# A newly searched order of one core's instructions, and warm-up matmuls on a tile of zeros, in a block-sparse attention and feed-forward kernel

## The chip, the cores and the metric

The kernel runs on one core of a Trainium2 chip. The metric is the device time of one execution in microseconds (us); lower is better. The core has several engines, each with its own queue of instructions which it executes in order: TensorE (PE, matrix products, with a separate row PEld for the loading of weights), VectorE (DVE), ScalarE (ACT), GpSimd (POOL) and SyncE (SP, which here only issues DMA transfers). Data come from the chip's memory (HBM) into SBUF by DMA; products land in PSUM.

## The reference

Inputs are q, k and v of shape 4 batches x 8 heads x 768 tokens x 64, and two weights, 512x2048 and 2048x512. Cut to what matters:

```python
k_rep = k.reshape(B, H, n_blocks, 64, D).mean(axis=3)          # 12 blocks of 64 keys
gate_scores = einsum('bhsd,bhnd->bhsn', q, k_rep)              # masked to causal blocks
top_idx = argsort(gate_scores)[..., -3:]                       # 3 best blocks of a query
scores = scale * q @ k.T       # kept only in the chosen blocks and the query's own, causal
attn = softmax(scores)
x = (attn @ v).transpose(0, 2, 1, 3).reshape(3072, 512)
out = gelu_tanh(x @ w_in) @ w_out
```

## The kernel before, in words

The 32 heads are worked on as 16 pairs, p = 0 to 15, four pairs to a batch b. For each pair `load` (L375 on) brings k, q and v by SP's queue: `first` issues one part and `others` the rest, and for pairs from 4 on k and q take four DMAs each (L396) and v two (L390). `pre` prepares a pair: k and q are turned (on TensorE for batch 0, L540 and L543; with DVE's transpose, L559, later), the block sums of k are taken (`ksb_h` L590, or `ks_all` L616 and `ksb_m` L633), the gate is computed by eight small matmuls (`gate`, L682), and DVE picks three blocks (L698, L705 to L719) and builds the additive mask `madd`, which a transpose (L751) or a transposing DMA (`mask_dma`, L758) turns. `heads2` (batch 0) and `heads` (batches 1 to 3) then compute the attention in units: scores into the PSUM tiles `wide` (L858, L1041), ACT's exponential (L877, L1054), POOL's causal cut (L903, L1068), the product with v (L926, L1080) and DVE's division (L944; L963 and L964). `turn_out` turns the result into xT (L983, or a DMA, L988).

The feed-forward of a batch has two stages. `s1` multiplies xT with w_in (L1117, groups of eight matmuls into `wide`, each followed by ACT's gelu, L1129); the last batch uses `s1_seven` (L1206, L1230, L1165). The second stage is a plain product with w_out for batch 0 (`s2_plain`, L1317, stores at L1342) and for the others one with seven block products in place of eight (`s2`, L1367), whose sums and differences DVE forms in the tiles XS and TS (`sums`, L1304; `w_sums`, L1286) and adds up (L1416). The weights come by POOL's DMA queue (`load_w`); an SP instruction, `hold` (L1562), waits for the second half of w_in before pair 4's loads go out. Batch b's second stage shares TensorE with the attention of batch b+1.

`consts` has POOL write constants: the causal tables, and for each of four buffer sets the memsets of `emit_p` (L505 to L509; L507 clears the first 128 columns of mT2[i], the turned masks, whose tiles are parts of XS). An identity matrix is built by POOL, and DVE casts it to `ident16` (L280). `warm` (L1514 on) defines up to 72 warm-up matmuls, 128x128 on 128x256, whose results nobody reads; L1519 in the profile.

None of this runs in the order of the text. Each step is an op, given to a planner with `add`: on which engines it may run, at what cost, behind which ops, with what priority. A search outside of the kernel has used these costs, and its result stands in three tables: ORDER (L21), the list of op numbers in the order in which they are emitted; BUFFER, which of several equal buffers each op takes; ENGINE, which ops go to ACT or POOL when they have a choice (the rest go to the first engine named, mostly DVE). `Plan.run` goes through ORDER and emits op after op. Every engine executes its own ops in that order, and waits inside its queue for whatever an op depends on. The costs themselves emit nothing. Ops 0 to 1889 are the real ones, 1890 on the warm-ups; ORDER holds 26 of these.

Op numbers that the text uses: 974 is `ksb_m` of pair 8, 977 the gate of pair 8, 1039 the DVE transpose of pair 9's q, 1040 the gate of pair 9; 450, 468 and 524 are output stores of batch 0; 408 to 411 are a group of the first stage that reads the second half of w_in; 337 and 338 are the casts of pair 4's k.

Of the kernel before, what the change touches and what calls it, by code (L numbers as in the profile page):

```python
# [9 lines left out]
FP16 = mybir.dt.float16  # L10
# [178 lines left out]
    "POOL": [  # L189
        337, 338, 586, 587, 646, 647, 707, 708, 972, 973, 1035, 1036,  # L190
        1097, 1159, 1160, 1426, 1489, 1613]}


class Op:
# [40 lines left out]
def kernel(  # L235
# [9 lines left out]
    nc = tc.nc  # L245
# [6 lines left out]
    HP = H // 2  # L252
# [1369 lines left out]
```

## Time and profile before

| what | us |
|---|---|
| median of 3 runs | 258.84 (258.12 to 259.08) |
| the profiled execution's own time | 258.29 |
| its span in the trace | 256.6 |
| PE busy in the span | 246.3 (96%) |
| DVE, ACT, POOL busy | 193.6, 174.1, 85.2 |
| first matmul of all starts at | 2.27 |
| first matmul of the feed-forward (L1117) | 37.61 |

The span is 1.7 us shorter than the execution's time; the rest lies around it. In the profile L12 is line 12 of the kernel. A timeline row is: start, duration, engine, line, operation, what it writes and reads, and in square brackets how long the engine had idled before it and what released it. "SPq" is SP issuing a DMA, not the transfer itself. "PEclk" is the granted clock of TensorE in tenths.

### The profile page before, as it was taken

The page shows a single profiled execution, that of the slowest core. Times are in us where ns is not written, and L with a number is a line of the kernel's source. Part 1 is how long each engine was busy: PE and PEld are TensorE (multiplying, and loading weights), DVE is VectorE, ACT ScalarE, POOL GpSimd, SP SyncE. Part 2 cuts the span into 40 slices and gives each one's busy share as a digit, 9 for nine tenths or more (in the row PEclk, how much of TensorE's full clock was granted, in tenths as well). Part 3 has the DMA queues.
Part 4 walks back from the last instruction along what each step waited for, and adds up shares of the span by engine and source line. Part 5 has one row for each costly group of instructions (what it writes and reads, how often), then busy time and mean ns, then how long its engine had stood idle before and what let it go on. Part 6 is the DMA issues. An engine that isn't in the chain of part 4 may idle for free.

```text
span 256.6 us, 6416 instructions
## 1 busy us (share of the span) xinstructions
PE 246.3 (96%) x2472; PEld 171.1 (67%) x2472; DVE 193.6 (75%) x542; ACT 174.1 (68%) x220; POOL 85.2 (33%) x165
## 2 busy tenths in 40 slices
PE   6999999999999996999999999999999999999994
PEld 5766676655455564555777888656777787666883
DVE  1688871032899995998999998998898773668954
ACT  2489886444789896767888874556898956576300
POOL 8448860012055966030173754000075520000000
PEclk9999999999999999999999999999999999999999
DMA  8998599999998998999999994153110321021024
GB/s 162 218 201 171 86 211 188 213 153 151 159 136 143 158 208 124 172 154 225 181 140 206 197 120 79 28 179 100 26 43 2 64 74 41 1 80 45 4 82 164
DMA packets 130927, 32.62 MB, mean 127 GB/s; under 512 B 124528, under 2 KB 126928, under 8 KB 130896
## 3 DMA queue, kind: packets, MB, share of 16 engines
q1 hardware_dynamic: 126160, 27.62, 64.3%
q0 software_dynamic: 3136, 4.19, 9.7%
q10 hardware_dynamic: 1600, 0.39, 0.8%
q8 instruction: 19, 0.31, 0.5%
q14 instruction: 12, 0.10, 0.1%
HBM read 27.26 MB, written 6.29 MB: 131 GB/s over the span
## 4 chain that ended last, share of the span: by engine, by line
PE 69%; DVE 17%; ACT 3%; DMA 3%; issue 2%; SPq 2%; POOL 2%; DVEq 0%; ACTq 0%; POOLq 0%
PE wide L1117 18%; PE bank L1367 17%; PE wide L1041 6%; PE bank L1317 5%; PE wide L1206 5%; PE bank L1080 4%; PE wide L858 3%; DMA sd<-in_q_dram 3%; DVE XS L1304 3%; DVE sel L714 2%; PE bank L682 2%; DVE G L1304 2%; PE bank L926 2%; PE bank L540 2%; DVE qT L363 2%
## 5 line engine op out<-in xcount | busy, mean ns | idle before, releaser
L1117 PE MATMUL wide<-xT,w_in 128*128 128x384 f16 x416 | 73.7, 326 | 0.0
L1054 ACT ACTIVATE ats<-wide 128x896 f16<-128x896 f32 x72 | 62.9, 916 | 8.0 <-PE wide L1041 6.0
L1129 ACT ACTIVATE G<-wide 128x768 f16<-128x768 f32 x52 | 41.9, 810 | 30.5 <-PE wide L1117 30.2
L1117 PEld LDWEIGHTS <-w_in 128*128 128x128 f16 x416 | 40.0, 98 | 26.2 <-issue 1.0
L1068 POOL TENSOR_SCALAR_AFFINE_SELECT ats<-ats 128x256 f16<-128x256 f16 x72 | 33.2, 477 | 68.4 <-ACT ats L1054 67.8
L1041 PE MATMUL wide<-qT,kT 76*128 76x512 f16 (+3 forms) x192 | 38.9, 305 | 0.2 <-ACT ats L1054 0.2
L559 DVE STREAM_TRANSPOSE s<-sd 128x768 f32<-128x768 f32 x24 | 23.2, 968 | 18.5 <-DMA sd<-in_k_dram 13.4
L1367 PE MATMUL bank<-w_out,G 128*128 128x256 f16 x216 | 33.1, 273 | 0.7 <-DVE G L1304 0.3
L1367 PEld LDWEIGHTS <-G 128*128 128x128 f16 x288 | 26.9, 98 | 7.2 <-DVE G L1304 0.8
L1317 PE MATMUL bank<-w_out,G 128*128 128x512 f16 x96 | 27.6, 379 | 0.0
L1080 PEld LDWEIGHTS <-ats 128*128 128x128 f16 x504 | 22.2, 98 | 5.0 <-issue 0.5
L1416 DVE TENSOR_TENSOR osb<-bank,osb 128x512 f32<-128x512 f32 (+1 forms) x38 | 22.4, 593 | 3.5 <-PE bank L1367 1.8
L1080 PE MATMUL bank<-v,ats 128*128 128x65 f16 x504 | 24.1, 194 | 0.4 <-DVE osb L1416 0.4
L1041 PEld LDWEIGHTS <-kT 76*128 76x128 f16 x192 | 17.2, 98 | 10.4 <-issue 1.3
L1367 PE MATMUL bank<-TS,XS 128*128 128x256 f16 x144 | 23.1, 272 | 0.0
L1367 PEld LDWEIGHTS <-XS 128*128 128x128 f16 x216 | 20.0, 97 | 4.2
L877 ACT ACTIVATE ats<-wide 128x1024 f16<-128x1024 f32 (+3 forms) x24 | 20.9, 921 | 2.1 <-PE wide L858 1.0
L361 POOL CAST kT<-s 64x768 f16<-64x768 f32 x18 | 15.3, 854 | 20.9 <-DVE s L559 17.2
L361 POOL CAST v<-vsd 128x768 f16<-128x768 f32 x13 | 11.8, 906 | 20.6 <-DMA vsd<-in_v_dram 20.5
L964 DVE TENSOR_TENSOR xn<-bank,zr 128x384 f16<-128x384 f32 x24 | 13.4, 557 | 0.8
L714 DVE MAX8 sel<-sel 128x8 f32<-128x12 f32 x160 | 13.3, 157 | 0.6
L1317 PEld LDWEIGHTS <-G 128*128 128x128 f16 x96 | 8.8, 97 | 6.3 <-issue 0.8
(119 smaller groups left out, 359.0 us busy)
## 6 DMA issues: line engine op xcount, KB each, us to landing
out_dram<-osb SPq DMA_DIRECT2D x23, 256.0 KB
vsd<-in_v_dram SPq DMA_DIRECT2D x26, 192.0 KB
sd<-in_k_dram SPq DMA_DIRECT2D x48, 96.0 KB
sd<-in_q_dram SPq DMA_DIRECT2D x48, 96.0 KB
w_in<-in_moe_w_in_dram POOLq DMA_DIRECT2D x2, 1024.0 KB, 11.5
w_out<-in_moe_w_out_dram POOLq DMA_DIRECT2D x2, 1024.0 KB, 17.2
G<-in_k_dram SPq DMA_DIRECT2D x4, 192.0 KB
G<-in_q_dram SPq DMA_DIRECT2D x4, 192.0 KB
```

The lines of the kernel that those rows point to most:

```text
L361: nc.gpsimd.tensor_copy(out=out, in_=in_)
L559: nc.vector.transpose(out=T[key + "T32", p], in_=T[key, p].rearrange("p t j -> p (t j)"))
L877: nc.scalar.activation(out=T["at", u][:, :, 0:n], in_=plan.buf[("st",) + u].rearrange("p (h w) -> p h w", h=2)[:, :, 0:n], func=AF.Exp, bi ...
L1041: nc.tensor.matmul(st[:, x:e], kT16[i][h][0:76, s0:s0 + 128], qT16[i][h][0:76, s0 + (x - cb):s0 + (e - cb)], start=True, stop=True)
L1054: nc.scalar.activation(out=T["at", u][:, 0:n], in_=plan.buf[("st",) + u][:, 0:n], func=AF.Exp, bias=0.0, scale=SCALE)
L1068: nc.gpsimd.affine_select(out=dg, in_=dg, compare_op=ALU.is_ge, fill=0.0, base=0, pattern=[[0, 2], [1, 128]], channel_multiplier=-1)
L1080: nc.tensor.matmul(pvv[:, qc, 0:65], at[:, cb + (qc - jc) * 128: cb + (qc - jc + 1) * 128], v16[i][:, jc, h, :], start=(gi == 0 and jc == ...
L1117: nc.tensor.matmul(hps[:, 512 * e:512 * e + HALF], w_in16[:, ci, (2 * j + e) * 128: (2 * j + e + 1) * 128], T["xT", b][:, ci, HALF * h:HAL ...
L1129: nc.scalar.activation(out=G[:, :, h, j, :], in_=plan.buf["hps", b, j, h].rearrange("p (e w) -> p e w", e=2)[:, :, 0:HALF], func=AF.Gelu_a ...
L1317: nc.tensor.matmul(plan.buf["ops", b, ti], G[:, f % 2, 2 * ti // NC, f // 2, ti % (NC // 2) * 128:ti % (NC // 2) * 128 + 128], w_out16[:, ...
L1367: nc.tensor.matmul(dst[:, HD * h:HD * h + HD], FACT[m][0][:, j, t * 128:(t + 1) * 128], FACT[m][1][:, j, :], start=(clear and j == 0), sto ...
L1416: nc.vector.tensor_tensor(out=dst(), in0=src(), in1=other(), op=ALU.add)
```

## The change

The three tables are replaced by those of a search that went on. The real ops are the same 1890, in another order, with other buffer picks and some on other engines; warm-ups grow from 26 to 39. The planner's costs for loads of pairs from 7 on are raised (2.9 for 2.5, 2.0 for 1.77). The warm-up matmuls read `zero16`, a part of XS[2], which the first instruction of VectorE sets to zero, in place of the identity; that part is the one that `emit_p` cleared for i = 3, so POOL leaves this memset out. XS is allocated further up for it. Lines behind that place are some 5 higher in the changed kernel (L540 is L545, L682 is L687, L1117 is L1122, L1519 is L1524).

```diff
 ORDER = [
-    6, 4, 0, 2, 3, 1, 9, 12, 15, 1890, 1891, 1892, 1893, 1894, 1895, 1896,
-    1897, 1898, 1899, 62, 71, 72, 64, 82, 63, 18, 22, 23, 19, 1900, 1901,
-    66, 75, 73, 68, 76, 26, 74, 67, 1902, 1903, 1904, 78, 31, 32, 35, 27,
+    6, 0, 4, 2, 1890, 1891, 1892, 1893, 1894, 1895, 1896, 1897, 1898,
+    1899, 1900, 1901, 1902, 1903, 1904, 62, 9, 63, 64, 15, 3, 1, 71, 72,
+    12, 1905, 1906, 73, 75, 74, 76, 77, 1907, 1908, 66, 18, 1909, 1910,
+    1911, 1912, 1913, 84, 68, 19, 22, 23, 26, 31, 195, 67, 78, 93, 82, 79,
...
-    744, 745, 1036, 746, 523, 1086, 1039, 974, 734, 977, 758, 830, 747,
-    1043, 756, 748, 749, 1037, 831, 978, 759, 832, 760, 761, 544, 539,
-    833, 1040, 969, 1083, 762, 1035, 979, 540, 1090, 752, 834, 1095, 1087,
...
+    739, 737, 974, 686, 725, 740, 741, 1033, 729, 627, 733, 532, 743, 533,
+    1034, 534, 738, 535, 536, 742, 537, 538, 744, 734, 1037, 745, 539,
+    746, 977, 628, 966, 687, 1039, 1040, 1028, 756, 830, 747, 544, 1082,
...
 ENGINE = {
     "ACT": [
-        63, 67, 72, 74, 85, 90, 101, 110, 114, 119, 139, 345, 349,
-        449, 467, 486, 504, 523, 541, 580, 594, 597, 655, 657, 658,
-        719, 749, 893, 980, 981, 1043, 1044, 1106, 1167, 1382, 1496,
-        1497, 1668, 1674, 1677, 1698, 1704, 1707, 1727, 1736, 1786,
-        1822],
+        67, 72, 74, 85, 90, 94, 101, 110, 114, 121, 130, 134, 141,
+        329, 331, 345, 346, 348, 449, 467, 486, 504, 523, 541, 580,
+        595, 597, 628, 657, 658, 718, 893, 929, 980, 981, 1043, 1044,
+        1106, 1167, 1202, 1434, 1559, 1668, 1674, 1677, 1698, 1704,
+        1707, 1727, 1736, 1786, 1822],
     "POOL": [
-        337, 338, 586, 587, 646, 647, 707, 708, 972, 973, 1035, 1036,
-        1097, 1159, 1160, 1426, 1489, 1613]}
+        586, 587, 646, 647, 707, 972, 973, 1035, 1036, 1097, 1098,
+        1159, 1160, 1425, 1489, 1551, 1612]}
...
+    NJ = NF // 2
+    XS = [persist.tile([128, NJ, HALF], FP16, name=f"XS_{x}")
+          for x in range(3)]
+    zero16 = XS[2][:, 2 * HP - 2, 0:128]
+    nc.vector.memset(zero16, 0.0)
...
         move = add({"DMA": 0.6 if (key, p) == ("k", HP) else
-                    2.5 if dve else 1.77}, lambda _: None, [go],
+                    2.5 if dve and p < 7 else 2.9 if dve else 1.77 if p < 7 else 2.0}, lambda _: None, [go],
...
-                nc.gpsimd.memset(mT2[i][:, 0:128], 0.0)
+                if i < HP - 1:
+                    nc.gpsimd.memset(mT2[i][:, 0:128], 0.0)
...
     def warm():
-        z = ident16.unsqueeze(1).to_broadcast([128, 2, 128])
-        prev = add({"NONE": 0.0}, lambda _: None, [], -1e6, lag=1.3)
+        z = zero16.unsqueeze(1).to_broadcast([128, 2, 128])
+        prev = add({"NONE": 0.0}, lambda _: None, [], -1e6, lag=0.25)
         for n in range(NWARM):
             def emit(_, n=n):
-                nc.tensor.matmul(plan.buf["warm", n][:, 0:256], ident16, z,
+                nc.tensor.matmul(plan.buf["warm", n][:, 0:256], zero16, z,
                                  start=True, stop=True)
```

BUFFER changes with ORDER, entry by entry; it is not shown.

More of the change, by code (lines that the diff above doesn't have):

```diff
@@ L298 @@
         nc.vector.memset(ksb3[i], 0.0)
-    NJ = NF // 2
     G = persist.tile([128, 2, 2, NJ, HALF], FP16, name="G")
-    XS = [persist.tile([128, NJ, HALF], FP16, name=f"XS_{x}")
-          for x in range(3)]
     TS = persist.tile([128, 3, NJ, DM // 2], FP16, name="TS")
```

302 rows, old and new, of tables (BUFFER, ORDER) are left out of this document.

## The prediction

> **What bounds the kernel now.** I read the page's sums and slices first, then PE's waits, then the table of 20 us stretches, then the timeline where the long waits are.
>
> ```profile
> span 256.6 us, 6416 instructions
> ...
> PE 246.3 (96%) x2472; PEld 171.1 (67%) x2472; DVE 193.6 (75%) x542; ACT 174.1 (68%) x220; POOL 85.2 (33%) x165
> ...
> PEclk9999999999999999999999999999999999999999
> ```
>
> The waits of TensorE (what waited, for whom: us in total, times, longest):
>
> ```profile
> PE bank L1519 <- DVE ident L280: 2.3, 1, 2.3
> PE bank L682 <- DVE zr L963: 2.1, 1, 2.1
> PE bank L1080 <- DVE osb L1416: 0.4, 1, 0.4
> ```
>
> Stretches of 20 us: length, then busy us of PE, PEld, DVE, ACT, POOL with their instructions, granted clock, DMA share, GB/s:
>
> ```profile
> 20.00:40.00 20.00, 19.71 (x357) 14.65 (x354) 15.84 (x56) 18.13 (x23) 14.69 (x28) 1.00 0.86 159
> 40.00:60.00 20.00, 20.00 (x124) 11.74 (x122) 4.01 (x6) 10.07 (x14) 1.32 (x2) 1.00 1.20 181
> 60.00:80.00 20.00, 19.80 (x159) 10.40 (x158) 14.55 (x54) 15.72 (x22) 6.97 (x12) 1.00 1.20 134
> 80.00:100.00 20.00, 19.22 (x236) 11.98 (x234) 16.93 (x41) 17.45 (x23) 13.91 (x27) 1.00 1.04 175
> 100.00:120.00 20.00, 18.46 (x138) 10.59 (x139) 18.33 (x56) 13.95 (x18) 3.41 (x4) 1.00 1.14 177
> 120.00:140.00 20.00, 19.58 (x188) 14.45 (x187) 19.47 (x56) 17.02 (x21) 6.84 (x11) 1.00 1.10 171
> 140.00:160.00 20.00, 20.00 (x258) 16.40 (x256) 18.73 (x38) 14.35 (x17) 12.25 (x23) 1.00 1.00 142
> ```
>
> TensorE is busy for 96% of the span at a full granted clock, so only three things can move the time: the start, TensorE's idle time, and other work put on its queue. Between 40 and 160 us TensorE idles 0 + 0.20 + 0.78 + 1.54 + 0.42 + 0 = 2.94 us (20 less PE's sum), and one wait of 2.1 us, at L682, is most of it. DVE is nearly full from 100 to 160 us, ACT from 20 to 40, and the DMA share is at or over 1.0 from 40 to 160: loads are paced by the DMA engines there, and come no earlier for being wanted earlier.
>
> **The 2.1 us wait.** The timeline around it:
>
> ```profile
> 91.94 0.53 SPq L390 DMA_DIRECT2D vsd<-in_v_dram  x1
> ...
> 92.56 0.49 SPq L396 DMA_DIRECT2D sd<-in_q_dram  x1
> ...
> 93.15 0.47 SPq L390 DMA_DIRECT2D vsd<-in_v_dram  x1
> ...
> 93.67 3.82 SPq L396 DMA_DIRECT2D sd<-in_q_dram  x3
> ...
> 99.03 0.38 PE L1080 MATMUL bank<-v,ats 128*128 128x65 f16 x7
> ...
> 99.81 0.98 DVE L559 STREAM_TRANSPOSE s<-sd 128x768 f32<-128x768 f32 x1 [2.54 <-DMA sd<-in_q_dram]
> ...
> 100.71 0.62 DVE L633 TENSOR_TENSOR ksb<-bmask,ks 128x32 f32<-128x32 f32 x1
> ...
> 101.47 0.48 PE L682 MATMUL bank<-s,ksb 128*32 128x160 f32 x8 [2.06 <-DVE zr L963]
> ...
> 105.38 0.48 PE L682 MATMUL bank<-s,ksb 128*32 128x160 f32 x8
> ```
>
> From the page's DMA issues, bytes of one issue:
>
> ```profile
> out_dram<-osb SPq DMA_DIRECT2D x23, 256.0 KB
> vsd<-in_v_dram SPq DMA_DIRECT2D x26, 192.0 KB
> ```
>
> TensorE's work ends at 99.03 + 0.38 = 99.41. The gate of pair 8 (op 977) then waits for `ksb_m` (op 974, L633), which stands in DVE's queue behind the transpose of pair 9's q (op 1039, L559). DVE idled 2.54 us for that q's load. So pair 8 waits for a transfer that it doesn't use. The waits view names zr L963, DVE's last work before the start; the true cause is one place ahead of it.
>
> In the new ORDER 974 stands at place 622, gate 977 at 648, transpose 1039 at 652: gate 8 no longer waits for q9. But gate 9 (op 1040) is now at 653, directly behind on TensorE's in-order queue, where it was at 105.38, four us later. So the same load is what is late next. SP now issues q9 ahead of two v loads that it had around it (91.94 and 93.15). At the 175 GB/s of the stretch 80:100, 2 x 196,608 bytes take 2.2 us, so q9 lands at about 99.8 - 2.2 = 97.6 and its transpose ends near 98.6, against a TensorE that arrives at 99.41 or shortly after. The margin is about 0.8 us. Term: -2.06; bounds: -2.06 (nothing waits) and, if the two loads had shared the engines with q9 all along and nothing is won, DVE is done at 99.81 + 0.98 = 100.8 as before, TensorE waits 1.4 of the 2.06 (-0.66). I take -2.06, nearer to the SP rows, which show q9's issue spread over 4.9 us, from 92.56 to 97.49, with a v load inside.
>
> The planner's longer loads (2.9 for 2.5, 2.0 for 1.77, pairs from 7 on) emit no instruction: they act through the table alone.
>
> **The start.** From the timeline:
>
> ```profile
> 0.89 0.06 DVE L282 MEMSET identk<- 128x2 f32 x1 [0.89 <-PEq L1606]
> ...
> 1.90 0.20 POOL L507 MEMSET XS<- 128x128 f16 x1
> ...
> 1.99 0.23 DVE L280 CAST ident<-identk 128x128 f16<-128x128 f32 x1 [0.29 <-POOL identk masks.py:199]
> ...
> 2.27 2.31 PE L1519 MATMUL bank<-ident 128*128 128x256 f16 x10 [2.27 <-DVE ident L280]
> ...
> 4.40 1.64 PE L540 MATMUL bank<-identk,G 128*128 128x130 f32 x6
> ...
> 6.72 0.48 ACT L359 COPY s<-bank 128x384 f32<-128x384 f32 x1 [2.45 <-PE bank L543]
> ...
> 6.90 1.48 PE L540 MATMUL bank<-identk,G 128*128 128x130 f32 x6
> ...
> 8.95 0.49 PE L1519 MATMUL bank<-ident 128*128 128x256 f16 x3
> ...
> 11.11 0.89 PE L540 MATMUL bank<-identk,G 128*128 128x130 f32 x6
> ...
> 12.99 1.74 ACT L877 ACTIVATE ats<-wide 128x512 f16<-128x512 f32 x2
> ```
>
> The warm-ups need the identity, which DVE casts at 1.99 from what POOL builds; TensorE starts at 2.27. With a tile that DVE zeroes at 0.89 it can start near 1.1. It then issues 15 instead of 10: each takes 2.31 / 10, near 0.21 us, together 3.2, so they end near 4.3, just before the first real matmul (4.40, which waits for the first load). That start does not move. What can move is the moment of the full clock. Six L540 take 1.64 and 1.48 us at 4.4 and 6.9, and 0.89 at 11.11: the speed doubles between 6.9 and 8.95, some 5.8 us after TensorE's start. Shifted by 2.27 - 1.1 = 1.2, it would come near 7, and about half of 1.2 us of slow work is saved: -0.6 at most, 0 at least. What follows is ACT's: it is busy 18.13 of 20 us from 20 to 40, and the new ENGINE table gives it, before its last early exponential, five half copies (94, 121, 130, 134, 141) and takes three (63, 119, 139). Net two x 0.48 = +0.96 of ACT, which an earlier first exponential (12.99) has to pay for, and the gaps ahead of it can (2.45 at 6.72). Term for the whole stage: -0.3; bounds -0.6 and +0.96. POOL is spared one memset of 0.20 (L507), and pair 4's two k casts (337, 338) go from POOL to DVE, which has room to 60 us (4.01 of 20): nothing for either.
>
> On warm-up the Trainium skill, "TensorE: Matmul & The Clock Gate", section "Part 1: The HAM clock gate", says that the clock is raised after a busy window of about 3.4 us which runs freely, not from the kernel's first matmul, and that the ramp is under 1% of a span and not to be tuned by counts. By it the 1.2 us could buy nothing or one window. This trace's 5.8 us from first matmul to full speed fits one window missed and one filled; that hangs on one run.
>
> **The rest of the order.** Behind pair 9 the ENGINE table takes eight copies or casts from DVE (929, 1202, 1434, 1559 to ACT; 1098, 1425, 1551, 1612 to POOL) and gives it five (1382, 1496, 1497, 1426, 1613).
>
> ```profile
> 135.37 0.39 PE L1367 MATMUL bank<-w_out,G 128*128 128x256 f16 x2 [0.28 <-DVE G L1304]
> ...
> 193.13 0.69 DVE L1416 TENSOR_TENSOR osb<-bank,osb 128x512 f32<-128x512 f32 x1
> ...
> 193.88 0.37 PE L1080 MATMUL bank<-v,ats 128*128 128x65 f16 x7 [0.37 <-DVE osb L1416]
> ```
>
> Here DVE ends last (135.37, 193.88). Without q9's 2.54 us of idle, its chain to 135 comes about as much earlier as TensorE does, so the 0.28 stays; by 194 DVE has three copies fewer (L1416's 0.69 is a like one, together near 2 us), so the 0.37 goes. Term -0.3, bounds -0.65 and 0. Four more warm-ups than before stand after 40 us, some in stretches where TensorE has no idle time (20.00 of 20): half of 0.21 each at full speed, +0.44; bounds 0 and +0.44.
>
> The first feed-forward matmul, and SP's hold, which waits for the second half of w_in:
>
> ```profile
> 37.61 1.14 PE L1117 MATMUL wide<-xT,w_in 128*128 128x384 f16 x6
> ...
> 41.99 0.58 SPq L1562 DMA_DIRECT2D after_in<-w_in  x1
> ```
>
> The new table reads that half in the fourth of the feed-forward's groups of eight matmuls (ops 408 to 411). Six take 1.14 us, less where one overlaps the next, so three groups, 24, take 4 to 4.6: the fourth begins at 41.4 to 42, against 41.99 at which the half is known to be there: a wait of 0 to 0.6, I take +0.2. The first output store (op 450), 256 KB, goes from place 538 to 432, ahead of loads of pairs 6 to 8: 262,144 bytes at 134 GB/s (60:80) delay them by up to 2.0 us. TensorE idles 0.20 there, so they have had slack, of unknown size. Stores 468 and 524 move 70 and 79 places up on the same queue, with the same price each where loads are behind them. I take +0.3 for new waits of this and the like, bounds 0 and +2.0.
>
> **Sum.** -2.06 - 0.3 - 0.3 + 0.44 + 0.2 + 0.3 = -1.72 on a profiled execution of 258.29: 256.6. The median of three runs, 258.84, stands 0.55 above it; I predict 256.8, between 256.6 and 258.84 - 1.72 = 257.1. The bounds add to -3.3 and about +3.3 beside the gate's.
>
> **Rivals.**
> A. Gate 9 takes the wait of gate 8. With both together, TensorE waits until q9 has landed and been transposed. The store put forward (2.0 us) against the v loads put back (2.2) decides. From q9 landing at 98.4 on, each us late costs one; at 103.4 the wait is 5, 3 more than now: 258.29 + 3 = 261.3, the small terms at zero. For it: DMA share 1.04 to 1.20, so that no load can catch up. Against it: the v loads behind q9.
> B. No change. q10 and q11 land as before, so the next gate gives back what gate 8 won, and ACT what the start won: 258.29 - 0.3 + 0.44 = 258.4. For it: the DMA share; against it: TensorE idles only 0.42 us from 120 to 160.
> C. More goes: all 2.94 us of the middle, 0.6 at the start, 0.3 near 194: 254.5. Against it: TensorE's idle outside the 2.06 is many pieces of 0.2.
> D. The full clock comes no sooner, so ACT's +0.96 is paid by nothing: -2.06 + 0.96 - 0.3 + 0.44 + 0.2 + 0.3 = -0.46, 257.8. It is decided by the six L540 at 6.90: 1.48 us again, or about 0.9. This is what the free-running window of the Trainium skill's page above would do in one run of some.
>
> **How the numbers follow.** Chances: forecast 0.50; C 0.08; B 0.08; D 0.10; A and any other new wait like it 0.24. A measurement tells 0.5%, 1.3 us, from no change: faster is below 257.5 (forecast and C: 0.58), same from there to 260.1 (B, D and the mildest of A: 0.20), slower the rest of A: 0.22. The range leaves out half of C and the upper part of A, 260.8 being a wait of 2.5 us more than now: 254.9 to 260.8; the forecast's own is 255.3 to 257.5.
>
> **What would show it.** Right: no idle over 0.5 us before L682's gates at pairs 8 and 9 (now near L687); the L559 transpose for q9 before 99; first warm-up near 1.1 with a first exponential before 12.5; the first feed-forward matmul no later than 37.6. Wrong: a TensorE wait of over 1 us released by a DVE L559 or by a `sd` load between 60 and 120 us; ACT's last exponential later than now; a gap at the fourth feed-forward group near 41 us.

## The result and the profile after

The changed kernel takes 257.75 us (257.08 to 258.92, 22 runs) against 258.97 us before (256.81 to 259.97, 22 runs): a ratio of 0.9959, 95% interval 0.9943 to 0.9974. That is 0.4% or about 1.1 us less, where 0.8% was forecast: the sign was right and the size twice too large. The profiled executions stand 0.5 us apart, 257.76 against 258.29. Of 98 executions of the kernel before that were timed beside the experiments, 33 show a mean granted clock of 0.993 and take 259.07 to 260.08 us, and none of the changed kernel's 22 does; against the other 65 (0.998 to 1.000, median 258.46) the changed kernel gains about 0.7 us.

The page of the changed kernel, its waits of TensorE (us in total, times, longest), and the stretches that answer to those shown of before (busy us of PE, PEld, DVE, ACT, POOL; clock, DMA share, GB/s):

```profile
span 256.0 us, 6451 instructions
...
PE 246.5 (96%) x2485; PEld 171.2 (67%) x2485; DVE 191.4 (75%) x539; ACT 176.4 (69%) x225; POOL 84.3 (33%) x163
```

```profile
PE bank L756 <- DVE madd L724: 2.1, 2, 1.2
PE bank L1524 <- DVE bmask L292: 1.1, 1, 1.1
PE bank L548 <- DMA G<-in_q_dram: 0.8, 1, 0.8
PE bank L1372 <- DVE XS L1309: 0.7, 1, 0.7
PE bank L687 <- DVE XS L367: 0.5, 1, 0.5
```

```profile
20.00:40.00 20.00, 19.68 (x355) 14.71 (x353) 14.48 (x53) 18.29 (x25) 13.97 (x23) 1.00 0.85 159
40.00:60.00 20.00, 20.00 (x125) 11.87 (x124) 4.09 (x6) 11.36 (x15) 0.00 (x0) 1.00 1.21 182
60.00:80.00 20.00, 20.00 (x162) 10.62 (x161) 14.91 (x52) 16.14 (x22) 6.74 (x12) 1.00 1.06 162
80.00:100.00 20.00, 18.77 (x230) 11.89 (x229) 18.13 (x48) 17.42 (x23) 11.14 (x24) 1.00 0.95 132
100.00:120.00 20.00, 20.00 (x153) 11.63 (x151) 18.37 (x53) 14.43 (x19) 6.15 (x8) 1.00 1.19 185
120.00:140.00 20.00, 19.07 (x186) 14.00 (x183) 19.45 (x58) 16.00 (x21) 7.88 (x13) 1.00 1.11 145
```

The 2.1 us at the gate is gone (100:120 is full), and so is half of the first wait. But TensorE now idles 1.23 us in 80:100 and 0.93 in 120:140, where it idled 0.78 and 0.42. Idle shares don't tell how far the work has come, so the table below does. Every matmul of the trace, warm-ups left out, is given the median distance to the next start that its form has in the kernel before; the sum is 227.1 us of real work in both kernels. The rows say when each kernel had begun a given part of it. They are not exact: the eight small products of a gate count 0.06 us in this sum and take 0.48, so a row shifts where a gate stands ahead of it in one kernel and behind it in the other.

```
real work done   before   changed   difference
 26 us            39.23     39.75     +0.52
 62               77.13     78.11     +0.98
 68               83.99     85.47     +1.48
 80               97.09     98.36     +1.26
 86              106.50    105.30     -1.20
 98              119.15    117.33     -1.82
110              131.28    131.38     +0.10
122              144.26    143.92     -0.34
end              252.91    252.39     -0.52
```

So the stretch with the gates, 97 to 106 us, gave 2.46 us, a little more than the 2.06 of the wait alone. The changed kernel came there 1.26 us late, and lost its new lead again between 119 and 131. The table puts that loss at 1.9; but two gates (16 products, 0.91 us) stand ahead of the row of 98 in the kernel before and behind it in the changed one, and with 0.48 us for each eight of them the lead there is 1.2 and the loss 1.3. The experiments below look for these two losses.

### The profile page after: what moved, and what is told of

Read it like the earlier page. It is cut to its first block, busy times and chain, and to the rows that moved or that the text cites. A ratio compares the mean times of both kernels' runs of the same rounds, so it can differ in the third digit from the quotient of the medians.

```text
span 256.0 us, 6451 instructions
## 1 busy us (share of the span) xinstructions
PE 246.5 (96%) x2485; PEld 171.2 (67%) x2485; DVE 191.4 (75%) x539; ACT 176.4 (69%) x225; POOL 84.3 (33%) x163
## 3 DMA queue, kind: packets, MB, share of 16 engines
q1 hardware_dynamic: 126160, 27.62, 65.4%
## 4 chain that ended last, share of the span: by engine, by line
PE 51%; DVE 16%; SPq 11%; DMA 10%; POOL 4%; issue 3%; ACT 3%; ACTq 1%; DVEq 0%; POOLq 0%
PE bank L1372 17%; PE wide L1122 10%; SPq L400 9%; PE wide L1046 6%; PE wide L1211 5%; DMA w_in<-in_moe_w_in_dram 5%; PE bank L1085 5%; PE bank L1322 3%; DVE qT L367 3%; DMA sd<-in_k_dram 3%; DVE sel L719 2%; DVE s L564 2%; DVE XS L1309 2%; DMA G<-in_q_dram 2%; ACT ats L882 1%
## 5 line engine op out<-in xcount | busy, mean ns | idle before, releaser
L1122 PE MATMUL wide<-xT,w_in 128*128 128x384 f16 x416 | 72.6, 326 | 0.0
L1122 PEld LDWEIGHTS <-w_in 128*128 128x128 f16 x416 | 40.0, 98 | 26.8 <-issue 1.3
L1073 POOL TENSOR_SCALAR_AFFINE_SELECT ats<-ats 128x256 f16<-128x256 f16 x72 | 33.3, 475 | 60.3 <-ACT ats L1059 60.2
L1046 PE MATMUL wide<-qT,kT 76*128 76x512 f16 (+3 forms) x192 | 39.1, 305 | 0.1
L1372 PE MATMUL bank<-w_out,G 128*128 128x256 f16 x216 | 31.4, 272 | 0.0
L365 POOL CAST kT<-s 64x768 f16<-64x768 f32 x17 | 15.2, 891 | 37.5 <-DVE s L564 37.0
L1046 PEld LDWEIGHTS <-kT 76*128 76x128 f16 x192 | 17.3, 98 | 10.5 <-issue 0.8
L1372 PE MATMUL bank<-TS,XS 128*128 128x256 f16 x144 | 22.0, 272 | 0.8 <-DVE XS L1309 0.7
L365 POOL CAST v<-vsd 128x768 f16<-128x768 f32 x13 | 11.4, 875 | 13.8 <-DMA vsd<-in_v_dram 8.8
```

Source lines behind the costliest of these rows:

```text
L365: nc.gpsimd.tensor_copy(out=out, in_=in_)
L1046: nc.tensor.matmul(st[:, x:e], kT16[i][h][0:76, s0:s0 + 128], qT16[i][h][0:76, s0 + (x - cb):s0 + (e - cb)], start=True, stop=True)
L1073: nc.gpsimd.affine_select(out=dg, in_=dg, compare_op=ALU.is_ge, fill=0.0, base=0, pattern=[[0, 2], [1, 128]], channel_multiplier=-1)
L1122: nc.tensor.matmul(hps[:, 512 * e:512 * e + HALF], w_in16[:, ci, (2 * j + e) * 128: (2 * j + e + 1) * 128], T["xT", b][:, ci, HALF * h:HAL ...
L1372: nc.tensor.matmul(dst[:, HD * h:HD * h + HD], FACT[m][0][:, j, t * 128:(t + 1) * 128], FACT[m][1][:, j, :], start=(clear and j == 0), sto ...
```

## The experiments

Each time stands with its ratio to the kernel before, run in the same group, and its 95% interval. For the changed kernel itself this ratio is 0.9959. Two theories were set against each other at first: S, the prediction's own, by which every wait of TensorE counts in full; and C, by which the loads and DVE's nearly full queue set the time up to about 136 us, so that a wait that goes earlier is given back there.

**The gate's wait alone, in the kernel before.**

```diff
-    744, 745, 1036, 746, 523, 1086, 1039, 974, 734, 977, 758, 830, 747,
+    744, 745, 1036, 746, 523, 1086, 974, 1039, 734, 977, 758, 830, 747,
```

> The kernel before with one number moved: op 974 (ksb_m of pair 8) stands ahead of op 1039 (transpose of pair 9's q), so that gate 8 no longer waits for q9. Theory C (the loads on SP's queue and DVE's saturated queue behind them set the time up to about 136 us; a wait of TensorE ahead of that is given back there): the 2.06 us at L682 falls to 0.5 or less, waits of about the same sum come back by 136 us at products that DVE feeds (L1367), and the time falls by 0 to 0.5 us. Theory S (every wait of TensorE counts in full, as the prediction's sum took it): the time falls by 1.6 to 2.1 us.

258.41 us, 0.9993 (0.9971 to 1.0014): no difference. Its timeline (start, duration, engine, line; in brackets the idle time and what ended it):

```profile
98.55 0.98 DVE L559 STREAM_TRANSPOSE s<-sd 128x768 f32<-128x768 f32 x1 [1.93 <-DMA sd<-in_q_dram]
...
98.75 0.32 PE L682 MATMUL bank<-s,ksb 128*32 128x160 f32 x4
...
100.95 0.51 PE L983 MATMUL bank<-ident,xn 128*128 128x128 f16 x6 [1.12 <-DVE xn L964]
...
116.85 0.75 PE L682 MATMUL bank<-s,ksb 128*32 128x160 f32 x16 [0.76 <-DVE ksb L633]
...
143.00 0.39 PE L1080 MATMUL bank<-v,ats 128*128 128x65 f16 x7 [0.75 <-POOL ats L1068]
```

Gate 8 runs at 98.75 without the long wait, and 1.12 us of it are back two us later, at the next product that needs DVE, which still waits 1.93 us for q9 in its queue. More is given back at 116.85 and 143.00. That is theory C in the main, with the waits at other lines (L983, L682, L1080) than it named; the last of them comes behind 136 us and ends with POOL, not DVE. The run tests the swap alone: q9's load is late in it as before.

**The gate's order undone, in the changed kernel.** 974 goes behind 1039 again, and 977 behind it.

```diff
-    739, 737, 974, 686, 725, 740, 741, 1033, 729, 627, 733, 532, 743, 533,
+    739, 737, 686, 725, 740, 741, 1033, 729, 627, 733, 532, 743, 533,
...
-    746, 977, 628, 966, 687, 1039, 1040, 1028, 756, 830, 747, 544, 1082,
+    746, 628, 966, 687, 1039, 974, 977, 1040, 1028, 756, 830, 747, 544, 1082,
```

> The changed kernel with the order of the two DVE ops at the gates as before: 974 (ksb_m of pair 8) behind 1039 (transpose of pair 9's q), and gate 977 behind it. In the changed kernel q9 is there when DVE comes to 1039 (at 100.13, with no idle time). If the 2.06 us went because SP issues q9 ahead of the v loads: TensorE waits 0.4 to 0.7 us at the gates (0.28 in the changed kernel) and the time rises by 0.5 or less, to 257.7 to 258.2. If the swap of the two ops is what removed it: a wait of 1.5 us or more comes back and the time rises to 258.8 or more.

257.52 us, 0.9950 (0.9930 to 0.9969): no slower than the changed kernel. The wait before the gates is 0.97 us, more than the 0.4 to 0.7 expected, but far from 2.06:

```profile
100.65 0.96 DVE L564 STREAM_TRANSPOSE s<-sd 128x768 f32<-128x768 f32 x1
...
101.54 0.73 DVE L638 TENSOR_TENSOR ksb<-bmask,ks 128x32 f32<-128x32 f32 x1
...
102.32 0.47 PE L687 MATMUL bank<-s,ksb 128*32 128x160 f32 x7 [0.97 <-DVE ksb L638]
```

DVE comes to q9's transpose without idle time. SP has issued the whole of q9 by 92.4 us in the changed kernel, where the kernel before issues its last piece at 97.49:

```profile
90.15 2.25 SPq L400 DMA_DIRECT2D sd<-in_q_dram  x4
```

So about half of the 2.06, 1.1 us, went because q9's load is there in time. The swap of the two ops is worth nothing in the time: with it undone, TensorE's 0.72 us of idle time before 126.71 are gone instead.

**Pair 6's choice of blocks.** TensorE's new wait at 81.74 ends with DVE's `madd`. One of pair 6's two q casts, which the change had moved from ACT to DVE, stands ahead of it. First it goes back to ACT (`ENGINE["ACT"]` gets 655).

> The changed kernel with one op put back from DVE to ACT (655, one of pair 6's two q casts), which stands in DVE's queue ahead of the choice of blocks of pair 6 and makes TensorE wait 1.2 us at 81.74 (L756 for madd L724). The wait falls to 0.4 or less. S: the time falls by 0.8 to 1.0 us below that of the changed kernel, to about 256.8. C: it is given back by 130 us at L1372, and the time stays at 257.5 to 257.8.

256.93 us, 0.9922 (0.9897 to 0.9947): theory S here, about 0.8 us below the changed kernel. L756's wait falls to 0.7 in total; a new one of 0.5 for ACT (L1046, at 78.4) appears, where the cast now is. A variant that is told with the combinations below left both casts on DVE, only behind the choice, and its wait stayed. So DVE's order was not the whole cause. In the changed kernel a DVE instruction of the choice is stretched while POOL works without a pause, on a causal cut (L1073) and a cast (L365):

```profile
79.97 0.40 POOL L1073 TENSOR_SCALAR_AFFINE_SELECT ats<-ats 128x256 f16<-128x256 f16 x1
80.22 1.06 DVE L720 TENSOR_TENSOR sel<-sel,sel 128x120 f32<-128x120 f32 x1
...
80.33 0.82 POOL L365 CAST v<-vsd 128x768 f16<-128x768 f32 x1
...
81.32 0.37 DVE L724 SCALAR_TENSOR_TENSOR madd<-sel,ownm 128x120 f16<-128x120 f32 x1
...
81.74 0.45 PE L756 MATMUL bank<-ident,madd 128*128 128x128 f16 x5 [1.20 <-DVE madd L724]
```

All seventeen L720 of the changed kernel, as minimum, median and maximum in ns:

```profile
L720 DVE TENSOR_TENSOR sel<-sel,sel x17: 234/283/1062, 8.8 to 175.7; 128x120 f32<-128x120 f32 x15, 128x48 f32<-128x48 f32 x1, 128x72 f32<-128x72 f32 x1
```

Of the fifteen of 128x120, the ten beside which no POOL instruction runs take at most 0.28 us; the five others take 0.28 to 1.06.

**The POOL cast moved.**

```diff
-    503, 705, 657, 665, 643, 578, 606, 507, 508, 565, 579, 661, 658, 509,
-    620, 616, 647, 617, 706, 510, 621, 625, 603, 707, 511, 512, 666, 504,
+    503, 705, 657, 665, 578, 606, 507, 508, 565, 579, 661, 658, 509, 620,
+    616, 643, 647, 617, 706, 510, 621, 625, 603, 707, 511, 512, 666, 504,
```

> The changed kernel with one POOL op moved: pair 6's v cast (643, at 80.33) goes three causal cuts later, behind op 616. In the changed kernel DVE's L720 of pair 6 lasts 1.06 us beside it, where the median of its seventeen is 0.28. If POOL's cast holds that DVE instruction up: L720 takes 0.6 us or less there, TensorE's wait at 81.74 (1.2) falls to 0.7 or less, and the time falls by 0.3 to 0.7 us, to 257.1 to 257.4. If it is only DVE's queue (the q cast 655) that is late: L720's length and the wait stay, 257.6 to 257.9.

257.05 us, 0.9938 (0.9916 to 0.9959). With the cast gone from beside it, the instruction takes 0.28:

```profile
80.02 0.80 POOL L1073 TENSOR_SCALAR_AFFINE_SELECT ats<-ats 128x256 f16<-128x256 f16 x2
...
80.27 0.28 DVE L720 TENSOR_TENSOR sel<-sel,sel 128x120 f32<-128x120 f32 x1
80.59 0.37 DVE L724 SCALAR_TENSOR_TENSOR madd<-sel,ownm 128x120 f16<-128x120 f32 x1
...
81.01 0.45 PE L756 MATMUL bank<-ident,madd 128*128 128x128 f16 x5 [0.43 <-DVE madd L724]
...
81.81 0.83 POOL L365 CAST v<-vsd 128x768 f16<-128x768 f32 x1
```

That shows it: a POOL cast moved by 1.5 us took 0.78 us off a DVE instruction, 0.77 off TensorE's wait, and 0.7 off the time (0.5 by the ratios). The Trainium skill, "SBUF — State Buffer", section "Who interferes with whom", says that a DVE instruction with two inputs in SBUF contends with a GpSimd instruction that reads SBUF, and that the ports which they share are an exclusive lock. The trace agrees for the cast: L720 has two such inputs and took 1.06 us beside it, while DVE's transposes of 128x768 (0.93 to 0.98 us, 13 of 24 beside POOL) don't stretch. It doesn't agree for every POOL instruction: with the cast moved, two causal cuts from 80.02 on, which read SBUF too, lie over the whole of L720, and it takes 0.28. Which of the two came first can't be told, since spans on POOL are rough.

**SP's queue ahead of k11.** A transposing DMA (982) of 2.69 us of issue stands ahead of most of k11's load.

```diff
-    1042, 1095, 839, 828, 811, 812, 829, 813, 982, 1091, 1094, 814, 1148,
-    1145, 487, 1149, 505, 815, 787, 788, 548, 789, 790, 806, 773, 549,
+    1042, 1095, 839, 828, 811, 812, 829, 813, 1091, 1094, 814, 1148, 1145,
+    982, 487, 1149, 505, 815, 787, 788, 548, 789, 790, 806, 773, 549,
```

> The changed kernel with one SP op moved: the transposing DMA of pair 8's mask (982, 2.7 us of issue at 106.57) goes behind the rest of pair 11's k load (1145). C: k11 lands some 2 us earlier than 115.2, DVE's idle 2.2 us before its transpose shrinks by 1.5 or more, TensorE's wait at 126.71 (0.9 and 0.24) shrinks to 0.3 or less, and the time falls by 0.6 to 1.0 us, to about 257.0. Rival: the wait at 126.71 comes from the order of DVE's own ops (two choices of blocks ahead of the sums), the idle moves elsewhere, and the time stays within 0.2 us of the changed kernel's.

257.05 us, 0.9927 (0.9901 to 0.9954), 0.7 us below the changed kernel, as theory C said. The changed kernel:

```profile
106.57 2.69 SPq L763 DMA_TRANSPOSE mT<-madd  x1
...
110.51 1.83 SPq L400 DMA_DIRECT2D sd<-in_k_dram  x3
...
115.19 0.98 DVE L564 STREAM_TRANSPOSE s<-sd 128x768 f32<-128x768 f32 x1 [1.23 <-DMA sd<-in_q_dram]
```

and with 982 moved:

```profile
111.23 1.27 SPq L763 DMA_TRANSPOSE mT<-madd  x1
...
113.77 0.98 DVE L564 STREAM_TRANSPOSE s<-sd 128x768 f32<-128x768 f32 x1
```

k11's transpose comes 1.4 us earlier and DVE does not idle for it. The idle time was 1.23, not the 2.2 that the expectation named, and TensorE's waits for DVE's sums at 126 shrink from 0.7 in total to 0.3. (The row names in_q as the releaser, which is inferred; the op at this place in DVE's order is the transpose of pair 11's k.)

**Warm-ups.** Nine of the changed kernel's, between 50 and 72 us, are left out (1916 to 1924 in ORDER); then the six of the kernel before between 48 and 58 us (1907 to 1912).

> The changed kernel without the nine warm-up matmuls between 50 and 72 us (five behind op 440, three ahead of pair 4's gate, one ahead of pair 5's). Each takes 0.11 us of a TensorE that is never idle there. If they lie on the path: TensorE is 0.7 to 1.0 us further at 75 us, and the time falls by 0.5 to 1.0 us. If what was late behind them (the loads of pairs 5 and 6, and DVE's work on these) is late anyway, TensorE waits for the same sum at L687 or L756 before 82 us and the time stays within 0.2 us.

> The kernel before without its six warm-ups between 48 and 58 us (0.11 us each on a TensorE without idle time). If such warm-ups are a plain addition to the path, as nine were in the changed kernel (1.2 us less): 0.5 to 0.8 us less than before. If they stood where something else was late: TensorE's waits at 76.3 and 101.5 grow by the same sum and the time stays within 0.2 us.

256.55 us, 0.9918 (0.9890 to 0.9945), 1.2 us below the changed kernel; and 257.62 us, 0.9948 (0.9925 to 0.9971), 1.3 below before. Both are gains of about the size of the matmuls themselves (9 x 0.11 and 6 x 0.11): the second's interval reaches from 0.7 to 1.9 us, and against the 258.46 of the section on the result it is 0.8. In the table of real work the changed kernel without the nine stands at 77.25 for 62 us, 0.86 ahead of the changed kernel: most of the 0.98 that it had lost by there, to a kernel which has six of its own.

**The zero tile.** The kernel before with the zero tile and 15 warm-ups at the start; then the changed kernel with the identity and ten.

```diff
-        z = ident16.unsqueeze(1).to_broadcast([128, 2, 128])
+        z = zero16.unsqueeze(1).to_broadcast([128, 2, 128])
...
-                nc.tensor.matmul(plan.buf["warm", n][:, 0:256], ident16, z,
+                nc.tensor.matmul(plan.buf["warm", n][:, 0:256], zero16, z,
```

> The kernel before with the zero tile alone: warm-ups read zero16 that DVE's first instruction clears, POOL leaves its memset out, and 15 in place of 10 warm-ups stand at the start; the rest of the three tables as before. Both theories: first matmul near 1.07, TensorE at full speed by the first L545-like product near 4.3. S: the first exponential comes 1 us or more earlier and the time falls by 0.6 to 1.2 us. C: ACT's queue and the arrival of w_in (SP's hold near 42.0) do not move, and the time falls by 0 to 0.3 us.

> The changed kernel with the old warm-up: identity in place of the zero tile, ten at the start in place of fifteen, POOL's memset back. First matmul near 2.0 to 2.3, ten warm-ups end near 4.5. If the zero tile is worth what the prediction's term had (0.3) or more: 258.0 to 258.6. If the moment of the full clock is a matter of the run and the stage waits for DVE and ACT anyway: 257.5 to 257.9, no difference that can be told.

258.91 us, 0.9995 (0.9975 to 1.0016), and 257.66 us, 0.9961 (0.9939 to 0.9982): nothing either way. The moment of the full clock differs from run to run. The first six products of k start at 4.25 to 4.62 us in all kept traces. They took 1.64 us in the kernel before, 1.19 in the kernel before with its gate swapped, 1.59 in the kernel before with the zero tile, 1.64 in the changed kernel with the identity, and 0.91 in the changed kernel:

```profile
1.07 3.34 PE L1524 MATMUL bank<-XS 128*128 128x256 f16 x15 [1.07 <-DVE bmask L292]
...
4.25 0.91 PE L545 MATMUL bank<-identk,G 128*128 128x130 f32 x6
...
12.50 1.03 ACT L882 ACTIVATE ats<-wide 128x1024 f16<-128x1024 f32 x1
...
38.45 1.79 PE L1122 MATMUL wide<-xT,w_in 128*128 128x384 f16 x10
```

0.91 is full speed from the first product on, 1.64 half speed throughout. Over the sixteen kept traces whose first matmul is at 1.07 the six took 0.91 to 1.64; over the four that begin at 2.08 to 2.28, 1.19 to 1.64. So an earlier first matmul did not fix the moment, as the Trainium skill's page of the prediction ("TensorE: Matmul & The Clock Gate", section "Part 1: The HAM clock gate") says of a window that runs freely. Nor did the moment matter for what follows: the feed-forward begins at 38.45 in the changed kernel, where the clock came first, and at 38.50 with the identity.

**ACT's copies.** First all eight early half copies back on their former engines.

> The changed kernel with the eight early half copies put back on the engines that they had before (94, 121, 130, 134, 141 to DVE, 63, 119, 139 to ACT). If ACT's queue, with 0.96 us more of copies, made the feed-forward begin late (first product with w_in at 38.45 against 37.61 before and 37.1 to 37.2 in two variants of the kernel before), it begins at 37.5 to 37.8 and the time falls by 0.3 to 0.8 us. If the new order itself, not the engine of the copies, holds ACT up, DVE's copies stand in the way of its other early work, the first product comes at 38.3 or later, and the time stays or rises by up to 0.5.

264.56 us, 1.0223 (1.0192 to 1.0254). Neither case: op 63, on ACT again, stands in the new order ahead of the second half of q's first load, which ACT's queue issues, and TensorE waits for that load. In this wait its granted clock falls to 0.50, at 9.7 us, and is back at 1.00 at 16.5.

```profile
6.09 0.48 ACT L363 CAST XS<-bank 128x384 f16<-128x384 f32 x1 [2.90 <-PE bank L545]
6.62 1.34 ACTq L428 DMA_DIRECT2D G<-in_q_dram  x2
```

```profile
12.15 0.45 PE L548 MATMUL bank<-identk,G 128*128 128x128 f32 x1 [5.38 <-DMA G<-in_q_dram]
```

The same eight with the edits 655 and 982 and without the nine warm-ups, where 63 stands ahead of the same load:

> All four edits on the changed kernel (655 to ACT, 982 behind 1145, the eight half copies back, nine warm-ups out). Adding: 255.0 to 255.6. If DVE's queue up to 136 us is the bound by then: 256.2 to 256.8, with waits of TensorE for DVE between 115 and 136 us of over 1.5 us.

262.04 us, 1.0128 (1.0098 to 1.0157), 2.5 us less than without the three edits, which gave 0.8, 0.7 and 1.2 alone. Then seven of the eight, without 63, and after that two copies that DVE seemed to have room for (134 and 329):

> The changed kernel with seven of the eight early half copies back on their former engines (94, 121, 130, 134, 141 to DVE, 119, 139 to ACT); 63 stays on DVE, since on ACT it stands ahead of a load of q that ACT's queue issues. If ACT's 1.44 us of copies more set the beginning of the feed-forward: first product with w_in at 37.0 to 37.8 in place of 38.45, time 256.9 to 257.4. If DVE's queue in this order cannot take them: waits of TensorE for DVE at L548, L687 or L756 before 36 us of over 0.8 us in sum more than in the changed kernel, and 257.7 or more.

> The changed kernel with two copies given from ACT to DVE: 134 (half of pair 3's k, at 28.19, where DVE idles from 26.0 to 27.3) and 329 (half of xT, between ACT's last early exponential and its table load). If ACT's queue sets the beginning of the feed-forward: the first product with w_in comes at 37.5 to 38.0 in place of 38.45 and the time falls by 0.4 to 0.9 us, to 256.9 to 257.3. If the order of the exponentials and not ACT's sum is what counts: 38.2 or later, and 257.5 or more.

258.13 us, 0.9976 (0.9957 to 0.9995), and 258.53 us, 1.0003 (0.9982 to 1.0023): neither is faster than the changed kernel (the first cannot be told from it, the second is slower), with the first product of the feed-forward at 39.00 and 38.94 in place of 38.45. In the first, TensorE waits 0.81 us for DVE at 19.14 (L548). With 1.44 and 0.96 us of copies fewer on ACT the moment came later, so ACT's sum of copies alone does not set it. What in the new order makes it come 1.2 us later than in three runs of the old one (37.13 to 37.25) stays open.

**Combinations.** 655 on ACT and 982 moved; then also without the thirteen late warm-ups, with the two casts on DVE behind the choice of blocks; with 655 on ACT in their place; with 134 and 329 on DVE too; and with POOL's cast 643 moved in place of 655.

> The changed kernel with the edits of the two runs that took 0.7 to 0.8 us off each (op 655 to ACT, op 982 behind 1145). If the two waits are in series on TensorE's queue the gains add: 256.1 to 256.4. If both come out of one bound, DVE's queue up to 136 us, they do not: 256.7 to 257.0.

> The changed kernel with pair 6's two q casts (654, 655) left on DVE but behind the choice of pair 6's blocks (653), op 982 behind 1145, and without the thirteen warm-ups behind the beginning of the feed-forward. The runs so far added: 256.2 for the first two kinds of edit, less 1.2 for nine warm-ups, less 0.4 for four more, less 0.4 for an ACT free of the cast (wait of 0.65 at 78.4): 254.0 to 254.9. If the gains overlap: 255.2 to 255.8.

> The changed kernel with op 655 on ACT, op 982 behind 1145, and without the thirteen warm-ups behind the beginning of the feed-forward: as the run that left 654 and 655 on DVE but behind 653, only with the cast on ACT. If that run lost to the place of the two casts (its waits at 80.7 and 84.1, 2.3 us together): 254.6 to 255.3. If the warm-ups and the two edits share one gain: 256.0 to 256.6.

> As the run before it in this list, with the two copies 134 and 329 on DVE too. If ACT sets the beginning of the feed-forward: 0.4 to 0.9 us below that run. If not: within 0.2 us of it.

> The changed kernel with POOL's cast 643 behind 616 (in place of the q cast on ACT), op 982 behind 1145, and without the thirteen late warm-ups. Adding: 254.9 to 255.5, near the 255.4 of the variant with the cast on ACT, with a wait of 0.4 at L756 near 80 in place of that variant's 0.65 at 77.6. If DVE beside POOL lengthens at another place instead, as when the q casts were moved: 256 or more.

In this order: 256.18 us, 0.9899 (0.9873 to 0.9926); 257.50, 0.9950 (0.9934 to 0.9966); 255.38, 0.9871 (0.9850 to 0.9892); 255.58, 0.9884 (0.9863 to 0.9905); 255.24, 0.9861 (0.9830 to 0.9891). The first two gains add. The second kernel keeps little of the gains: with the casts out of the way, DVE's comparison comes earlier, into a stretch in which POOL has no pause from 77.92 to 80.23 us, and takes 1.78 us:

```profile
77.92 0.81 POOL L364 CAST kT<-s 64x768 f16<-64x768 f32 x1
...
78.58 1.78 DVE L719 TENSOR_TENSOR sel<-sel,sel 128x120 f32<-128x120 f32 x1
78.69 0.40 POOL L1072 TENSOR_SCALAR_AFFINE_SELECT ats<-ats 128x256 f16<-128x256 f16 x1
79.05 0.82 POOL L364 CAST v<-vsd 128x768 f16<-128x768 f32 x1
...
80.74 0.45 PE L755 MATMUL bank<-ident,madd 128*128 128x128 f16 x5 [1.07 <-DVE madd L723]
```

With 134 and 329 on DVE nothing is won. The last is the lowest, though not to be told from the third: 1.4% below before, and about 2.5 us below the changed kernel, with three kinds of edit to its tables. Its real work is 2.84 us ahead of before in the row of 86 and 2.99 at the end, so what is won at the gates stays won there. Its page begins:

```profile
span 253.6 us, 6424 instructions
```

## Why the prediction was half right

**The gate, -2.06.** The row and the cause were right: gate 8 waited for a load that it doesn't use, and in the changed kernel TensorE has no idle time ahead of the two gates. Rival A did not happen; q9's transpose ran at 100.13, later than the "near 98.6" of the prediction, but only because DVE was busy, and TensorE came later too. What failed is the step from TensorE's wait to the time: "-2.06" was entered whole, with only +0.3 against it for waits that come back. The runs showed in its place that the lead of 1.2 us behind the gates is gone by 131 us (+0.10 in the table), and that the swap of the two ops is worth nothing in the time: 258.41 us (0.9993) with the swap alone in the kernel before, 257.52 against 257.75 with it undone in the changed kernel. DVE is busy for 65.4 of the 72 us from 64 to 136 in the kernel before, and what TensorE wins without DVE ending its work sooner was taken back at products that DVE feeds (100.95 and 116.85 there, 126.71 in the changed kernel). The prediction saw this for the 0.28 at 135 and not for the 2.06. Rival B, given 0.08, had named this mechanism, with the wrong transfers.

**New waits, +0.3.** This term was too small: TensorE lost 0.5 us at 81.74 and 1.3 between 119 and 131. Behind the first stood a POOL cast beside a DVE instruction (0.7 us in the time when it was moved), behind part of the second an SP issue of 2.69 us ahead of a load (0.7 us). The prediction priced the store and the swapped loads on SP's queue and did not look at the masks' transposing DMAs there, nor at POOL beside DVE at all, although the kernel before has such rows: its L633 of 0.62 us was quoted, beside a POOL cast from 100.46 on, where the median is 0.19:

```profile
L633 DVE TENSOR_TENSOR ksb<-bmask,ks x12: 142/186/857, 56.6 to 168.9; 128x32 f32<-128x32 f32 x12
```

**Warm-ups, +0.44.** The balance of four at 0.11 us is right by the count: behind 40 us the kernel before has nine and the changed one thirteen. The runs price the two sides, not the balance: the nine of the middle are worth 1.2 us, the six of the kernel before 0.8 to 1.3. What the prediction did not ask is what leaving all of them out would give.

**The start, -0.3.** This term had the wrong sign. Measured +0.5 at 39 us (against a profiled execution of before whose full clock came late; three other runs of the old order stood 0.4 to 0.5 ahead of it there). The first matmul came at 1.07, as forecast, and the first exponential at 12.50, at the edge of the "before 12.5", but the first product of the feed-forward at 38.45 and not before 37.6. The full clock was there at 4.25 in the profiled run, earlier than the 7 forecast, and bought nothing. The price of ACT's copies (0.96) was not confirmed as the cause, which stays open. So rival D, whose 257.8 is the measured time, met it by luck: the full clock did come sooner.

**The w_in half, +0.2.** No wait is seen: the fourth group begins at 42.51, the hold at 41.60. **DVE's relief behind 135, -0.3**: the waits at 135.37 and 193.88 are gone or shorter, and the lead grows from -0.34 at 144 us to -0.52 at the end, as forecast.

The sum hit the sign because the gate's gain was larger than what was lost, and missed the size because it added a gain on TensorE that DVE's queue takes back, and took the start for a gain. Its upper bounds beside the gate's add to 4.0 (0.96 + 0 + 0.44 + 0.6 + 2.0), not to the 3.3 that it gives, and its -3.3 holds the gate's 2.06.

## What to carry to other kernels

Ask of each wait that goes whether the engine that ends it will also be done sooner: where its queue was full, as DVE's here, the time fell only by less work, shorter instructions or fewer idle stretches. Look for instructions that last several times their median beside another engine's, and move the other one: here one POOL op moved by 1.5 us took 0.5 to 0.7 us off. Warm-up matmuls inside a stretch where TensorE never idles were plain work here; leave them out and measure.

## What the runs showed of the hardware that was not expected

A DVE comparison of two SBUF tiles, 0.28 us alone, took 1.06 us beside one of POOL's casts of 0.8 us, and 1.78 over two of them with a causal cut between. The issue of a transposing DMA held SP's queue for 1.20 to 2.69 us. And the first six products of k, at nearly the same place 3.2 us and more behind a first matmul at 1.07, ran at full speed in some runs (0.91 us) and at half speed in others (1.64); a first matmul 1.2 us earlier did not make the full clock reliably earlier.
